# An attention stage moved from column tiles to 64x64 tiles of TensorE, two head pairs at a time

## The chip, the cores and the metric

One NeuronCore of one Trainium2 chip runs the whole kernel in one launch. The metric is the device time of that core in microseconds (us); smaller is better. The kernel before takes 602.62 us as the median of 3 runs (602.19 to 602.64).

## The reference

```python
S = q.shape[2]                               # q, k, v: (4, 12, 448, 64) float32
scores = q @ k.T / sqrt(64) - log(S)
attn = 1 / (1 + exp(-scores))                # a sigmoid: no sum over keys
attn_out = attn @ v
x = attn_out, tokens as rows                 # (1792, 768)
xn = x / sqrt(mean(x * x) + 1e-6) * rms_g
g, val = xn @ w_gate, xn @ w_val             # 768 -> 1536
out = (silu(g) * val) @ w_out                # 1536 -> 768
```

## The kernel before, in words

The kernel has three stages: attention (with the normalisation of its result), a gated feed-forward layer, and the output projection. Products run in float16 with each float32 operand split into a high part and a low part ("hi" and "lo"); three products (hi hi, hi lo, lo hi) then stand for one float32 product. The feed-forward stage uses Strassen-like sums of blocks, which is why a normalised activation is needed in seven combined forms (slots 0 to 6). Only the product of attention weights and v is done in float32 by TensorE itself. Each float32 matmul of the program shows as two MATMUL instructions in the trace.

**Attention.** The work unit is a pair of heads (24 pairs: 4 batches of 6). `load_qk` (L190, L191) brings q and k of a pair as 128 partitions by 7 chunks by 64; `load_v` (L199) brings v into slots with zero blocks between them. VectorE (DVE in the trace) makes hi (`qk_hi`, L204) and lo (`qk_lo`, L209) side by side, so that a 128-column chunk holds [lo | hi] of q and [hi | lo] of k. The chunks are transposed, for the first three pairs by TensorE against an identity (L224, evicted at L229 by VectorE and L231 by ScalarE), for the others by a DMA transpose on the SP queue (L214). After this, partitions 0 to 63 hold one part of the head dimension and 64 to 127 the other. `q_up` (L241) copies q's hi part to the lower partitions of a third plane whose upper half is zero.

`scores` (L258) handles a pair in four groups g. A 64-key block of a head is two matmuls over all 128 rows: one adds hi lo and lo hi at once (the two parts are stacked along the rows), one is hi hi against the zero half. Each matmul fills 64 of the 128 output partitions, and two of them on the two column halves of TensorE belong together. Groups 0 to 2 have 8 matmuls, group 3 has 4, so a pair has 28. One sigmoid on ScalarE (ACT, L260) evicts a group from PSUM. `av` (L271) multiplies with v, two float32 matmuls per group, again on the two column halves. After group 3 ScalarE evicts the result twice, squared (L280) and scaled by rms_g (L281), and VectorE later adds up the squares (L284).

**Order.** The program order is written out by hand: scores of two groups, then `av` of the two groups before them. Scores have two PSUM buffers. Between them `run_later` spends a budget (0.75 of VectorE per call, 0.18 of ScalarE) on queued parts: the adds of squares, `norm` (L302 sums, L307 to L323 a reciprocal square root, L329 spreads it, L332 scales, L336 and L341 split into hi and lo, L352 block sums) and the splitting of the first weights (`split_w`). What the budget has not reached at the end of attention stays in a list; parts beyond the last 33 (`N_NORM`) are issued at once ahead of the first feed-forward product, the last 33 between the products (`LEFT`).

```python
for n in range(0, len(todo) + 2, 2):
    for i, g in todo[n : n + 2]:
        scores(i, g)
        for part in FILL[g]:
            part(i)
        run_later()
    for i, g in todo[max(n - 2, 0) : n]:
        av(i, g)
        run_later()
while len(later) > N_NORM:
    later.pop(0)[0]()
```

Of the kernel before, what the change touches and what calls it, by code (L numbers as in the profile page):

```python
# [16 lines left out]
SQ = 2.0**6  # L17
# [7 lines left out]
def attention_then_swiglu(  # L25
# [27 lines left out]
    MID = S // P  # L53
    NG = MID + 1
# [15 lines left out]
    SPLIT_AT = 10  # L70
    ON_PE = 3
# [21 lines left out]
    NV = 10  # L93
    A_WORDS = 5 * 2 * S + 3 * NV * D + 4 * S
    B_WORDS = 2 * S + 3 * NCC * S + 3 * NK * S
# [23 lines left out]
    LDW, TW = 2 * NSLOT * D, 3 * NSLOT * D  # L119
    ld_b = [words(xc_room, XW + n * LDW, 2, NSLOT, D) for n in range(4)]  # L120
    nat_b = [words(xc_room, XW + 4 * LDW + n * LDW, 4 * NSLOT, D, dt=F16) for n in range(2)]
    nat_hi = [t[:, 1:-1].rearrange("p (t u) d -> p t u d", t=2)[:, :, 0::2] for t in nat_b]
    t_b = [words(xc_room, XW + 6 * LDW + n * TW, 3, NSLOT, P, dt=F16) for n in range(3)]
    at0 = 0
    a_b = [words(room, at0 + n * 2 * S, 2, S) for n in range(5)]
    at0 += 10 * S
    v_b = [words(room, at0 + n * NV * D, NV, D) for n in range(3)]
    at0 += 3 * NV * D
    sq_b = [words(room, at0 + n * S, S) for n in range(2)]
    at0 += 2 * S  # L130
    acc_b = [words(room, at0 + n * S, S) for n in range(2)]
    at0 += 2 * S
    diag_b = [words(room, at0 + n * S, S) for n in range(2)]
    at0 += 2 * S
# [46 lines left out]
    pairs = [(b, hp) for b in range(B) for hp in range(NPAIR)]  # L181
    at, pav = {}, {}

    def rows_of(src, i, order):
        b, hp = pairs[i]
        return src[b, 2 * hp : 2 * hp + 2].rearrange("h s d -> (h s) d").rearrange(order, p=P)

    def load_qk(i):
        t = ld_b[i % 4]
        nc.sync.dma_start(t[:, 0], rows_of(q, i, "(p c) d -> p c d"))  # L190
        nc.sync.dma_start(t[:, 1], rows_of(k, i, "(p c) d -> p c d"))  # L191

    def load_v(i):
        b, hp = pairs[i]
        t = v_b[i % 3].rearrange("p (j n) d -> p j n d", j=2)
        src = v[b, 2 * hp : 2 * hp + 2].rearrange("j (r c) d -> r j (c d)", c=NSLOT)
        for n in range(2):
            dst = t[64 * n : 64 * n + 64, :, 1 - n : 5 - n].rearrange("p j n d -> p j (n d)")
            nc.sync.dma_start(dst, src[:, :, MID * n * D : (MID * n + 4) * D])  # L199

    def qk_hi(i):
        nc.vector.tensor_scalar(nat_hi[i % 2], ld_b[i % 4], SQ, None, ALU.mult)  # L204

    def qk_lo(i):
        for t in range(2):
            lo = nat_b[i % 2].rearrange("p (t c l) d -> p t c l d", t=2, l=2)[:, t, :, t]
            stt(lo, ld_b[i % 4][:, t], SQ, nat_hi[i % 2][:, t], ALU.mult, ALU.subtract)  # L209

    def transpose(i):
        if i < ON_PE:
            return
        nc.sync.dma_start_transpose(  # L214
            out=t_b[i % 3][:, 0:2].rearrange("p t c r -> p (t c) r"),
            in_=nat_b[i % 2].rearrange("p u d -> p (u d)"),
        )

    def transpose_here(i, t, space, engines):
        nat = nat_b[i % 2].rearrange("p (t c l) d -> p t c (l d)", t=2, l=2)  # L220
        ps = space()
        for c in range(NSLOT):
            half_, at = divmod(c, MID + 1)
            nc.tensor.matmul(ps[half_][:, at * P : at * P + P], nat[:, t, c], ident16, start=True, stop=True)  # L224
        for half_, engine in enumerate(engines):
            n = MID + 1 - half_
            o = t_b[i % 3][:, t, half_ * (MID + 1) : half_ * (MID + 1) + n].rearrange("p c r -> p (c r)")
# [5 lines left out]
    def on_pe(i):  # L233
        if i < ON_PE:
            for t in range(2):
                transpose_here(i, t, lambda: [bank("tr") for _ in range(2)], (nc.vector, nc.scalar))
            credit[0] -= 1.1

    def q_up(i):
        T = t_b[i % 3]  # L240
        nc.vector.tensor_copy(T[:D, 2], T[D:, 0])  # L241

    def scores(i, g):

        T = t_b[i % 3]
        n = 1 if g == MID else 2
# [12 lines left out]
        a = at[i, g] = a_b[(i * NG + g) % 5]  # L259
        nc.scalar.activation(  # L260
            a[:, :n], ps[:, :n, :S], AF.Sigmoid, bias=bias_s, scale=1.0 / (math.sqrt(D) * SQ * SQ)
        )

    def av(i, g):
        b, hp = pairs[i]
        a = at.pop((i, g))
        if g == 0:
            pav[i] = bank("av")
        ps = pav[i]
        for j in range(2):  # L270
            nc.tensor.matmul(  # L271
                ps[64 * j : 64 * j + 64, :S],
                v_b[i % 3][:, NG + j if g == MID else 1 + 5 * j + g],
                a[:, 0 if g == MID else j],
                start=(g == 0),
                stop=(g == MID),
            )
        if g == MID:
            sq = sq_b[i % 2] if hp else acc_b[b % 2]
            nc.scalar.activation(sq, ps[:, :S], AF.Square)  # L280
            nc.scalar.activation(x_b[b % 3][:, hp], ps[:, :S], AF.Copy, scale=g_sb[:, hp : hp + 1])  # L281
            if hp:
                adds.extend([(wait, 0.0)])
                adds.append((lambda: tt(acc_b[b % 2], acc_b[b % 2], sq, ALU.add), 0.53))  # L284
            del pav[i]
# [4 lines left out]
    def norm(b):  # L290
# [4 lines left out]
        d = diag_b[odd][:TB]  # L295
# [144 lines left out]
    PARTS = ((0, 0), (0, 1), (1, 0))  # L440
# [275 lines left out]
    def ahead_by(n, part, cost=0.0):  # L716
        def run(i):
            if i + n < len(pairs):
                part(i + n)
                credit[0] -= cost  # L720

        return run

    FILL = (
        (ahead_by(1, on_pe), ahead_by(2, transpose)),
        (ahead_by(1, q_up, 0.4), ahead_by(5, load_qk)),
        (ahead_by(3, qk_hi, 0.53), ahead_by(2, load_v)),
        (ahead_by(3, qk_lo, 1.1),),
# [6 lines left out]
    for t in v_b:  # L735
        nc.vector.memset(t[:, NG : NG + 2], 0.0)
    for t in t_b:
        nc.vector.memset(t[D:, 2], 0.0)
# [186 lines left out]
```

## Time and profile before

| what | value |
|---|---|
| median of 3 runs | 602.62 us |
| the profiled execution: its own time | 603.15 us |
| its span in the profile | 601.3 us |
| end of the last `av` matmul (attention ends) | about 156.9 us |
| granted TensorE clock over the span | 1.00 |

PE is TensorE's matmuls, PEld its weight loads, DVE VectorE, ACT ScalarE, SP the queue that issues most DMAs. A row "xN | busy, mean" gives how many instructions a group has, the time that at least one of them ran, and the mean duration of one. Matmuls overlap, so a mean duration of 353 ns says nothing of the distance from one to the next; that is read from a stretch in which they stand back to back.

### The profile page before, as it was taken

The page shows a single profiled execution, that of the slowest core. Times are in us where ns is not written, and L with a number is a line of the kernel's source. Part 1 is how long each engine was busy: PE and PEld are TensorE (multiplying, and loading weights), DVE is VectorE, ACT ScalarE, POOL GpSimd, SP SyncE. Part 2 cuts the span into 40 slices and gives each one's busy share as a digit, 9 for nine tenths or more (in the row PEclk, how much of TensorE's full clock was granted, in tenths as well). Part 3 has the DMA queues.
Part 4 walks back from the last instruction along what each step waited for, and adds up shares of the span by engine and source line. Part 5 has one row for each costly group of instructions (what it writes and reads, how often), then busy time and mean ns, then how long its engine had stood idle before and what let it go on. Part 6 is the DMA issues. An engine that isn't in the chain of part 4 may idle for free.

```text
span 601.3 us, 9197 instructions
## 1 busy us (share of the span) xinstructions
PE 591.6 (98%) x3604; PEld 319.4 (53%) x3604; DVE 481.2 (80%) x763; ACT 265.0 (44%) x400; POOL 0.7 (0%) x6
## 2 busy tenths in 40 slices
PE   7999999999999999999999999999999999999997
PEld 5445454554455555555555555555556666666664
DVE  7696897986698998887887888878789997767651
ACT  5787887987553332323324324324232254222020
POOL 0000000000000000000000000000000000000000
PEclk9999999999999999999999999999999999999999
DMA  9999999972000330230320312303355014121112
GB/s 233 253 226 260 242 197 230 247 166 66 0 2 2 105 106 18 88 106 0 106 77 28 106 41 66 106 0 106 105 214 207 1 36 97 27 52 38 30 40 52
DMA packets 78747, 61.35 MB, mean 102 GB/s; under 512 B 42864, under 2 KB 77168, under 8 KB 78704
## 3 DMA queue, kind: packets, MB, share of 16 engines
q1 hardware_dynamic: 78384, 60.38, 39.2%
q8 instruction: 28, 0.46, 0.3%
q10 hardware_dynamic: 320, 0.39, 0.2%
q14 instruction: 15, 0.12, 0.1%
HBM read 45.62 MB, written 5.51 MB: 85 GB/s over the span
## 4 chain that ended last, share of the span: by engine, by line
PE 92%; ACT 3%; DVE 2%; DMA 2%; issue 1%; SPq 0%; ACTq 0%; DVEq 0%
PE cc L453 14%; PE cd L453 13%; PE ca L453 13%; PE o L542 12%; PE av L271 10%; PE sc L258 9%; PE cb L453 7%; PE oc L629 4%; PE od L629 4%; PE oa L629 4%; PE ob L629 2%; ACT room L260 1%; DMA room<-in_v_dram 1%; DMA xc<-in_k_dram 1%; ACT xc L336 1%
## 5 line engine op out<-in xcount | busy, mean ns | idle before, releaser
L453 PEld LDWEIGHTS <-wr 128*128 128x128 f16 x1512 | 147.8, 98 | 138.7 <-issue 1.2
L260 ACT ACTIVATE room<-sc,bias_s 128x896 f32<-128x896 f32 x96 | 83.9, 921 | 18.9 <-PE sc L258 18.5
L453 PE MATMUL ca<-xc,wr 128*128 128x448 f16 x432 | 89.6, 352 | 0.0
L271 PE MATMUL av<-room 128*64 128x448 f32 x384 | 80.7, 539 | 0.0
L258 PE MATMUL sc<-xc 128*64 128x448 f16 x672 | 74.0, 353 | 2.2 <-ACT room L260 1.1
L453 PE MATMUL cd<-xc,wr 128*128 128x448 f16 x324 | 67.2, 352 | 0.0
L453 PE MATMUL cc<-xc,wr 128*128 128x448 f16 x324 | 67.2, 352 | 0.0
L258 PEld LDWEIGHTS <-xc 128*64 128x64 f16 x672 | 40.7, 110 | 42.3 <-issue 25.4
L542 PE MATMUL o<-xc,room 128*128 128x384 f16 x354 | 58.3, 326 | 0.0
L481 ACT ACTIVATE room<-ca 128x448 f32<-128x448 f32 x24 | 13.0, 542 | 84.6 <-PE ca L453 84.6
L542 PEld LDWEIGHTS <-room 128*128 128x128 f16 x354 | 34.6, 98 | 22.9
L453 PE MATMUL cb<-xc,wr 128*128 128x448 f16 x216 | 44.8, 352 | 0.0
L271 PEld LDWEIGHTS av<-room 128*64 128x64 f32 x384 | 28.8, 137 | 27.1 <-issue 21.5
L429 DVE SCALAR_TENSOR_TENSOR wr<-wr 128x768 f16<-128x768 f32 (+1 forms) x48 | 39.1, 850 | 0.1
L508 ACT ACTIVATE room<-room 128x448 f32<-128x448 f32 x24 | 13.8, 576 | 53.4 <-DVE room L507 53.4
L426 ACT ACTIVATE wr<-wr 128x768 f16<-128x768 f32 (+1 forms) x48 | 34.2, 755 | 4.9 <-DVE wr L423 4.9
L476 DVE TENSOR_TENSOR room<-room,cb 128x448 f32<-128x448 f32 x24 | 14.9, 620 | 16.9 <-PE cb L453 16.8
L209 DVE SCALAR_TENSOR_TENSOR xc<-xc 128x448 f16<-128x448 f32 x48 | 27.8, 619 | 0.4
L381 DVE SCALAR_TENSOR_TENSOR wr<-wr 128x768 uint32<-128x768 uint32 x28 | 26.8, 957 | 0.8
L380 DVE SCALAR_TENSOR_TENSOR wr<-wr 128x768 uint32<-128x768 uint32 x28 | 26.8, 956 | 0.6
L469 ACT ACTIVATE room<-ca 128x448 f32<-128x448 f32 x24 | 13.0, 544 | 30.9 <-PE ca L453 25.2
L423 DVE TENSOR_TENSOR wr<-wr 128x384 f32<-128x384 f32 x48 | 25.6, 554 | 0.9
(145 smaller groups left out, 705.4 us busy)
## 6 DMA issues: line engine op xcount, KB each, us to landing
wr<-in_moe_w_gate_dram SPq DMA_DIRECT2D x36, 256.0 KB, 3.2
wr<-in_moe_w_val_dram SPq DMA_DIRECT2D x36, 256.0 KB, 3.9
room<-in_v_dram SPq DMA_DIRECT2D x48, 128.0 KB, 4.0
xc<-in_q_dram SPq DMA_DIRECT2D x24, 224.0 KB, 3.5
xc<-in_k_dram SPq DMA_DIRECT2D x24, 224.0 KB, 3.4
out_dram<-room SPq DMA_DIRECT2D x49, 96.0 KB, 2.2
wr<-in_moe_w_out_dram SPq DMA_DIRECT2D x6, 768.0 KB, 4.4
xc<-in_moe_w_out_dram SPq DMA_DIRECT2D x5, 768.0 KB, 6.3
```

The source lines that it names most:

```text
L209: stt(lo, ld_b[i % 4][:, t], SQ, nat_hi[i % 2][:, t], ALU.mult, ALU.subtract)
L258: nc.tensor.matmul(o, m, r, start=(w == 0), stop=(w == 1))
L260: nc.scalar.activation(a[:, :n], ps[:, :n, :S], AF.Sigmoid, bias=bias_s, scale=1.0 / (math.sqrt(D) * SQ * SQ))
L271: nc.tensor.matmul(ps[64 * j : 64 * j + 64, :S], v_b[i % 3][:, NG + j if g == MID else 1 + 5 * j + g], a[:, 0 if g == MID else j], start=( ...
L380: lambda: stt(b, r[:, :, 0], 29, b, ALU.logical_shift_right, ALU.bitwise_or),
L381: lambda: stt(b, r[:, :, 1], 0xC0000000, b, ALU.bitwise_and, ALU.bitwise_or),
L423: first.append((lambda o=o, f0=f0, f1=f1: tt(wf[:, o], wf[:, f0], wf[:, f1], ALU.subtract), 0.6))
L426: nc.scalar.activation(t[:, 0, s], wf[:, s], AF.Copy, scale=SW)
L429: stt(t[:, 1, s], wf[:, s], SW, t[:, 0, s], ALU.mult, ALU.subtract)
L453: nc.tensor.matmul(ps, w[:, l, b, c], xc[n, a][:, r, c], start=(not more and c == 0 and m == 0), stop=(c == NK - 1 and m == 2), skip_group ...
L542: nc.tensor.matmul(ps[:, :HALF], h[c, t // NTOK][:, l, t % NTOK * P : t % NTOK * P + P], wo[c][:, r, e * HALF : e * HALF + HALF], start=(c ...
L629: nc.tensor.matmul(ps[:, :HALF], a[x](m, l), b[y](m, r), start=(not more and m == 0 and n == 0), stop=(m == NFC // 2 - 1 and n == 2), skip ...
```

## The change

A unit is now two pairs of heads (12 units, 7 key chunks each, 84 steps in place of 96). Partitions 0 to 63 of q, k and v hold pair 0, partitions 64 to 127 pair 1; hi and lo are separate planes, and inside a chunk the two heads stand side by side, so that after the transposes a head's 64 dimensions fill one half of the partitions. A step issues 12 score matmuls of 64 rows by 64 columns (three products by two heads by two pairs) and 4 float32 `av` matmuls of the same size. Four matmuls in a row fall on the four quarters of TensorE; heads (score) or pairs (av) are the row halves, and these write different PSUM banks. The zero blocks of v and the copies of `q_up` are gone.

```diff
+    PARTS = ((0, 0), (0, 1), (1, 0))
-    def scores(i, g):
-        for j in range(2):
-            for w in range(2):
-                r = T[:, 2 * w, :, 64 * j : 64 * j + 64]
-                for half_ in range(2):
-                    cols = slice(64 * half_, 64 * half_ + 64)
-                    if g == MID and half_ != j:
-                        continue
-                    o = ps[cols, 0 if g == MID else j, :S].rearrange("p (c r) -> p c r", c=NSLOT)
-                    m = T[:, 1, MID if g == MID else g + NG * half_, 64 * j : 64 * j + 64]
-                    nc.tensor.matmul(o, m, r, start=(w == 0), stop=(w == 1))
+    def scores(u, c):
+        for n, (l, m) in enumerate(PARTS):
+            for j in range(2):
+                rows = slice(64 * j, 64 * j + 64)
+                for r in range(2):
+                    cols = slice(PB * r, PB * r + PB)
+                    o = ps[cols, j, :S].rearrange("p (c r) -> p c r", c=NSLOT)
+                    nc.tensor.matmul(
+                        o, T[rows, 1, l, c, cols], T[rows, 0, m, :, cols], start=(n == 0), stop=(n == 2)
+                    )
...
+        for r, ps in enumerate(pav[u]):
+            rows = slice(PB * r, PB * r + PB)
+            for j in range(2):
+                nc.tensor.matmul(
+                    ps[64 * j : 64 * j + 64, :S],
+                    v_b[u % 2][rows, j, c],
+                    a[rows, j],
...
+        evictions.extend((square, copy))
```

Around this: the four evictions of a unit (square and copy for two pairs) are issued one by one, each behind a `scores` or `av` (`run_evictions(1)`). Loads, hi, lo and transposes of q and of k are separate steps of a unit (`FILL`), two units ahead; `load_v` loads each value once. The first two units (four pairs, before: three) are transposed by TensorE, hi and lo apart; the first unit's loads come first, q before k. The hi copies of the normalisation of batch 1 go from ScalarE (15 of 448 columns) to VectorE (5 of 1344). The split of the second weights is queued at step 30, and weights from the third on are not loaded during attention:

```diff
-            if n < 8 or n % 4 == 0:
+            if True and loads and loads[0][0] < 2:
                 run_load()
-            if n == SPLIT_AT:
+            if n in SPLIT_AT:
...
+            if b == 1:
+                return [(lambda: nc.vector.tensor_copy(xc[n, slot][:, 0], f), 0.95)]
```

`N_NORM`, `LEFT` and both later stages are as before.

## Rows read from the trace of the kernel before

**Rows 1.** The page, part 1: busy time of each engine.

```profile
PE 591.6 (98%) x3604; PEld 319.4 (53%) x3604; DVE 481.2 (80%) x763; ACT 265.0 (44%) x400; POOL 0.7 (0%) x6
```

**Rows 2.** Busy time by stretch; last columns: granted clock, DMA share, GB/s.

```profile
0.00:16.90 16.90, 12.55 (x106) 8.73 (x108) 13.47 (x29) 8.85 (x13) 0.70 (x6) 1.00 0.95 238
16.90:156.90 140.00, 139.05 (x1043) 70.10 (x1043) 109.75 (x200) 117.31 (x172) 0.00 (x0) 1.00 0.89 199
...
30.00:60.00 30.00, 29.83 (x232) 14.98 (x228) 23.69 (x54) 24.80 (x35) 0.00 (x0) 1.00 1.08 244
```

**Rows 3.** The chain of waits, 15 to 30 us: start, length, what.

```profile
21.91 1.51 PE sc L258 x16
23.43 1.50 PE av L271 x8
```

**Rows 4.** Groups of instructions from 16.9 to 156.9 us.

```profile
L271 PE MATMUL av<-room 128*64 128x448 f32 x376 | 79.0, 539 | 0.0
L258 PE MATMUL sc<-xc 128*64 128x448 f16 x636 | 69.5, 353 | 0.9 <-ACT room L260 0.7
L260 ACT ACTIVATE room<-sc,bias_s 128x896 f32<-128x896 f32 x68 | 66.9, 1011 | 16.0 <-PE sc L258 15.5
L258 PEld LDWEIGHTS <-xc 128*64 128x64 f16 x636 | 38.5, 110 | 39.0 <-issue 24.4
L271 PEld LDWEIGHTS av<-room 128*64 128x64 f32 x376 | 28.2, 137 | 26.7 <-issue 21.1 <-ACT room L260 0.7
...
L260 ACT ACTIVATE room<-sc,bias_s 128x448 f32<-128x448 f32 x23 | 15.0, 651 | 0.0
...
L204 DVE TENSOR_SCALAR xc<-xc 128x896 f16<-128x896 f32 x20 | 12.5, 623 | 0.3
L336 ACT ACTIVATE xc<-room 128x448 f16<-128x448 f32 x21 | 12.3, 597 | 0.9 <-DVE room L352 0.8
...
L241 DVE COPY xc<-xc 64x896 f16<-64x896 f16 x22 | 8.6, 389 | 8.9 <-DMA xc<-xc 8.3
```

**Rows 5.** ScalarE in order of time: start, length, what.

```profile
70.78 1.92 ACT L260 ACTIVATE room<-sc,bias_s 128x896 f32<-128x896 f32 x2
...
73.02 0.58 ACT L280 ACTIVATE room<-av 128x448 f32<-128x448 f32 x1
73.45 0.68 ACT L281 ACTIVATE room<-av,g_sb 128x448 f32<-128x448 f32 x1
73.96 0.63 ACT L336 ACTIVATE xc<-room 128x448 f16<-128x448 f32 x1
```

**Rows 6.** The start in order of time: PE, then DVE, then ACT.

```profile
6.51 1.47 PE L258 MATMUL sc<-xc 128*64 128x448 f16 x8 [0.80 <-DVE xc L229]
...
5.17 1.29 DVE L229 CAST xc<-tr 128x512 f16<-128x512 f32 x2
...
7.37 0.63 DVE L204 TENSOR_SCALAR xc<-xc 128x896 f16<-128x896 f32 x1 [0.50 <-DMA xc<-in_k_dram]
8.04 1.16 DVE L209 SCALAR_TENSOR_TENSOR xc<-xc 128x448 f16<-128x448 f32 x2
...
14.09 0.63 DVE L204 TENSOR_SCALAR xc<-xc 128x896 f16<-128x896 f32 x1 [1.16 <-DMA xc<-in_k_dram]
...
3.86 0.58 ACT L759 ACTIVATE xc<-xc 128x448 f16<-128x448 f32 x1 [1.62 <-DMA xc<-in_k_dram]
```

**Rows 7.** SP's transposes: issue time min/median/max in ns, first and last start.

```profile
L214 SPq DMA_TRANSPOSE xc<-xc x21: 1378/2697/3816, 16.1 to 136.5; - x21
```

**Rows 8.** The end of attention in order of time: PE, then DVE.

```profile
156.90 1.88 PE L453 MATMUL ca<-xc,wr 128*128 128x448 f16 x9
...
163.41 0.99 PE L329 MATMUL rinv<-room,ones 112*128 112x448 f32 x2 [0.51 <-DVE room L323]
...
157.59 0.63 DVE L284 TENSOR_TENSOR room<-room 128x448 f32<-128x448 f32 x1 [2.43 <-ACT room L280]
158.58 1.56 DVE L341 TENSOR_TENSOR room<-room 128x1344 f16<-128x1344 f32 x1 [0.36 <-ACT room L336]
160.05 0.15 DVE L307 TENSOR_SCALAR m<-ssq 112x4 f32<-112x4 f32 x1
```

More of the change, by code (lines that the diff above doesn't have):

```diff
@@ L69, in attention_then_swiglu @@
     WARM = 9
-    SPLIT_AT = 10
-    ON_PE = 3
+    SPLIT_AT = (10, 30)
+    ON_PE = 2
+    MID = 3
     SLOT = 0.75
@@ L178, in attention_then_swiglu @@
     tt = nc.vector.tensor_tensor
-    pairs = [(b, hp) for b in range(B) for hp in range(NPAIR)]
     at, pav = {}, {}
[L184 to L199, printed above, removed]
@@ L203, in qk_hi, with rows_of @@
[L203 to L212, printed above, removed]
+    PARTS = ((0, 0), (0, 1), (1, 0))
+    def rows_of(src, u):
+        b, n = divmod(u, NPAIR // 2)
+        return [
+            src[b, 4 * n + 2 * r : 4 * n + 2 * r + 2].rearrange("j (p c) d -> p j (c d)", p=PB) for r in range(2)
+        ]
@@ new lines, in load, with load_qk, load_v, halves @@
+    def load(src, dst, u):
+        for r, rows in enumerate(rows_of(src, u)):
+            nc.sync.dma_start(dst[PB * r : PB * r + PB].rearrange("p j c d -> p j (c d)"), rows)
+    def load_qk(u, t):
+        load((q, k)[t], ld_b[u % 2][:, t], u)
+    def load_v(u):
+        load(v, v_b[u % 2], u)
+    def halves(u, t, l):
+        return nat_b[u % 2][:, t, l].rearrange("p c (j d) -> p j c d", j=2)
+    def qk_hi(u, t):
+        nc.vector.tensor_scalar(halves(u, t, 0), ld_b[u % 2][:, t], SQ, None, ALU.mult)
@@ L260, in scores, with av @@
         nc.scalar.activation(
-            a[:, :n], ps[:, :n, :S], AF.Sigmoid, bias=bias_s, scale=1.0 / (math.sqrt(D) * SQ * SQ)
+            a, ps[:, :, :S], AF.Sigmoid, bias=bias_s, scale=1.0 / (math.sqrt(D) * SQ * SQ)
         )
[L264 to L279, printed above, removed]
+    def av(u, c):
+        a = at.pop((u, c))
+        if c == 0:
+            pav[u] = [bank("av") for _ in range(2)]
+        for r, ps in enumerate(pav[u]):
+            rows = slice(PB * r, PB * r + PB)
+            for j in range(2):
+                nc.tensor.matmul(
+                    ps[64 * j : 64 * j + 64, :S],
+                    v_b[u % 2][rows, j, c],
+                    a[rows, j],
+                    start=(c == 0),
+                    stop=(c == NSLOT - 1),
+                )
+        if c == NSLOT - 1:
+            for r, ps in enumerate(pav.pop(u)):
+                evict(u, r, ps)
@@ L290, in norm, with run_evictions @@
+    def run_evictions(n):
+        for part in evictions[:n]:
+            part()
+        del evictions[:n]
+    evictions = []
     def norm(b):
@@ L714, in at_once, with ahead_by, run, next_v @@
         return [x for x in parts if x[0] is not wait]
[L716 to L719, printed above, removed]
+    def ahead_by(n, part, *t, cost=0.0):
+        def run(u):
+            if u + n < NU:
+                part(u + n, *t)
                 credit[0] -= cost
         return run
+    K, Q = 1, 0
+    def next_v(u):
+        if 0 < u < NU - 1:
+            load_v(u + 1)
     FILL = (
[L725 to L728, printed above, removed]
+        (ahead_by(2, qk_hi, K, cost=0.53),),
+        (ahead_by(2, qk_lo, K, cost=1.0),),
+        (ahead_by(2, transpose, K),),
+        (ahead_by(1, on_pe, K), next_v, ahead_by(2, qk_hi, Q, cost=0.53), ahead_by(4, load_qk, K)),
+        (ahead_by(2, qk_lo, Q, cost=1.0),),
+        (ahead_by(1, on_pe, Q), ahead_by(2, transpose, Q), ahead_by(4, load_qk, Q)),
+        (),
     )
@@ L764, in two_banks, with hi_on_act @@
             return [ps[:, n] for n in range(2)]
-        transpose_here(0, 0, two_banks, (nc.vector, nc.scalar))
-        transpose_here(0, 1, two_banks, (nc.vector, nc.scalar))
-        q_up(0)
-        for part in (qk_hi, qk_lo):
-            part(1)
-        load_qk(3)
-        todo = [(i, g) for i in range(len(pairs)) for g in range(NG)]
+        def hi_on_act(u, t):
+            nc.scalar.activation(halves(u, t, 0), ld_b[u % 2][:, t], AF.Copy, scale=SQ)
+        qk_hi(0, Q)
+        hi_on_act(0, K)
@@ new lines, in attention_then_swiglu @@
+        transpose_here(0, Q, 0, two_banks, (nc.vector, nc.scalar))
+        qk_lo(0, Q)
+        transpose_here(0, K, 0, two_banks, (nc.vector, nc.scalar))
+        qk_lo(0, K)
+        transpose_here(0, Q, 1, two_banks, (nc.vector, nc.scalar))
+        transpose_here(0, K, 1, two_banks, (nc.vector, nc.scalar))
+        for t in (K, Q):
+            qk_hi(1, t)
+            qk_lo(1, t)
+            transpose(1, t)
+            load_qk(2, t)
+        run_load()
+        run_load()
+        for t in (K, Q):
+            load_qk(3, t)
```

132 lines of the change are left out of this document (59 added, 73 removed).

## The prediction

> **What bounds the kernel now.** I read the shares first: PE is busy 98% of the span [rows 1]. The busy times by stretch then separate the stages: from 16.9 us to the end of attention at 156.9 us PE is busy for 139 of 140 us, ScalarE for 117, VectorE for 110, at a DMA share of 0.89, and the granted clock is 1.00, the 2.4 GHz level [rows 2]. So TensorE sets the pace of attention and ScalarE is next. The chain of waits alternates between scores and `av` with nothing between them [rows 3]; it gives the true cost of a matmul: 16 score matmuls in 1.51 us are 8 rounds of two column tiles at 189 ns; 8 `av` instructions in 1.50 us are 4 rounds at 375 ns. That two tiles share a round is seen, not assumed: the mean duration is 353 ns [rows 4], and yet one starts every 94 ns. In the dense stretch 636 score instructions times 94.4 ns and 376 `av` instructions times 187.5 ns [rows 4] make 130.5 us; the other 9.5 us are the normalisation's small matmuls and waits.
>
> **The change, part by part.**
>
> *Rounds on TensorE.* Before: 24 pairs x 28 scores x 94.4 ns = 63.4 us and 24 x 16 x 187.5 ns = 72.0 us, together 135.4. After: 84 steps, each with 12 score matmuls and 4 float32 matmuls (8 instructions). No row of this kernel shows two row tiles at work together, so the price of a round of four is bounded. Below: it streams the same 448 columns as a round of two, 189 and 375 ns. Above: only the column halves overlap, which doubles both. I take the lower end, because two tiles with separate streams already run at full rate [rows 3], and four streams over 64 partitions read as much as two over 128. That is 84 x (3 x 189 + 2 x 375) = 84 x 1.317 = 110.6 us: **-24.8 us** on the path. About 15.8 of it are the scores (three half-row products in place of two whole ones, of which one was half zeros), 9.0 the `av` products, whose fourth group ran with half a block of zeros.
>
> *Start.* Before, the first scores start at 6.51 us, and by 16.9 us 36 scores (672 less 636) and 8 `av` instructions are done, 4.9 us of work [rows 4, 6]. After, the first scores need q and k of two pairs. k of unit 0 is the third and fourth 224-KB transfer, and the fourth transfer of the kernel before has landed at 7.3 us, where `qk_hi` (L204) stops waiting [rows 6]. Then come in a row: hi on ScalarE, about 1 us (0.58 for half as many columns [rows 6]), the transposes, an eviction of 0.65 (half of 1.29 for two), lo 1.16, transposes and a last eviction: first scores at about 12 us. Unit 1's k is the eighth such transfer; the eighth landed at 14.1 us [rows 6], so its hi, lo and transposes hold TensorE again until about 21 us, with 4.9 us of work done by then (six steps of scores, two of `av`). That is **+4 us** (0 to +8). The four DMA loads of unit 0 and its two of v are issued ahead of everything else, so the weights and later loads only move back.
>
> *Waits inside the dense stretch.* Sigmoids have the same number of columns, but 84 instructions instead of 96. A second one adds 0.91 us to the first (1.92 less 1.01) [rows 4, 5], so 12 fewer starts save about 2 us. The hi copies of batch 1 leave ScalarE: 15 times some 0.5 us (0.59 with overlap [rows 4]) is 7.5, and 6 copies slide behind attention, 3 us. So 117 becomes about 105 us, in a stretch that shrinks from 140 to about 118: 89% in place of 84%. The evictions add 0.43 and 0.51 us each (starts 73.02, 73.45, 73.96 [rows 5]), four per unit, 1.9 us in a row of slots whose room is small: a round of two steps lasts 2.63 us on TensorE and takes 1.8 of sigmoid. The scores have two PSUM buffers, so a sigmoid late by more than half a microsecond stops TensorE. What is queued behind the evictions is the next sigmoid, and behind that the scores two steps on. I take 0.25 us per unit, **+3 us**; the bounds are -4 (the present 9.5 us shrink as the normalisation waits less) and +12 (1 us a unit).
>
> *VectorE, SP and DMA.* `q_up` goes, 8.6 us in this stretch [rows 4], and five casts come, each 1.5 times the 0.62 of L204 [rows 4], 4.7 us; VectorE stays under TensorE (about 103 of 118 us), so I cost both at nothing. If that cover goes, the late part is qk, with two units of slack. The DMA moves about 29 MB in place of 31.9 (238 GB/s x 16.9 and 199 x 140 [rows 2]): one transpose, the double v slots and the third weights fall away. At the share of before that is 128 us of DMA time in 139; 1.08 was held for 30 us [rows 2], so it is close but hidden. SP's 20 transposes hold its queue 2.7 us each [rows 7], 54 us; loads of the next units stand behind them, and both have 9 to 12 steps (12 us or more) until they are needed.
>
> *Behind attention.* The budget is spent per call of `run_later`: 192 calls before, 168 after. Following the credits through the loop, 35 parts are left before, and 44 after. So ahead of the first product stand eleven parts (two adds, a block sum, six hi copies, two lo) instead of two. TensorE's order holds the spread of the reciprocal root (L329), which waits for VectorE's chain from L307 on; it waits 0.51 us now, with 0.63 + 1.56 us of leftover ahead of that chain [rows 8]. One more add, one block sum and one lo are 0.63 + 1.55 + 1.56 = 3.7 us, and the second square lands an eviction later. The wait moves from 0.5 to about 4.5: **+4 us** (+0.5 if VectorE's chain overlaps ScalarE's, +6).
>
> *The rest* of the kernel is untouched. Sum: -24.8 + 4 + 3 + 4 = -13.8 us. The profiled execution took 603.15, which gives 589.3; the median of the runs shown lies 0.5 below that execution, so **589 us**. With the terms at their near ends together it is about 577, at their far ends 601.
>
> **The rivals.**
>
> *Slower: row halves do not overlap.* In `scores` and `av` the two row halves then take turns, and the change does not do what it says. Rounds cost 378 and 750 ns: +110.6 us, less some 4 of waits that get covered: about 695 us. The break-even lies where rounds are 13.8/110.6, an eighth, longer than 189 and 375 ns. Against it: row halves write different banks, as the column halves of `av` write different partitions. For it: no 64-row matmul stands in the trace. The Trainium skill, page "TensorEngine Tiling (Array Packing)", section "Tiling Modes", lists 64x64 as four tiles that work in parallel; no run here shows it yet. Chance 0.10.
>
> *Weight loads become the bound.* A round of two needs two loads in 189 ns, a round of four needs four. The 636 loads keep PEld busy 38.5 us, 61 ns each [rows 4]; four at that rate are 242 ns, so a score round costs 53 more: 84 x 3 x 53 = 13.4 us, 602 to 603, no change. `av` loads at 75 ns (28.2 / 376) would still hide. Against it: PEld is idle for 24.4 and 21.1 us there with nothing but its queue to wait for [rows 4], and the 61 ns include overlap. The Trainium skill, page "TensorE: Matmul & The Clock Gate", section "Part 3: Packing small matmuls — row/col tiling", measured 3.07 times for four row tiles, not 4. By that figure both kinds of round would be 1.3 times as long, and as an estimate the time would be about 622. By the trace, two column tiles lose nothing (two scores per 189 ns), so it is not borne out there. Chance 0.08.
>
> *ScalarE becomes the bound.* Each unit's four evictions push the sigmoids back by a full microsecond: +12 in place of +3, and with a start at +7 this is about 601. For it: 16.0 us of ScalarE's idle time is waiting for scores, so today it has room that the change takes [rows 4]. Against: the evictions are spread over four calls. Chance 0.08.
>
> **How the numbers follow.** The forecast has 0.74 and its time is the prediction. About 0.03 of that case lies under 577 and as much over 601; the second and third rivals end at 601 to 603, so 577 to 603 holds about 0.82 and leaves out the 695 and the tails. A measurement of this kernel tells about 0.2%, 1.2 us, from no change: faster is below 601.4, with nearly all of the forecast and half of the ScalarE rival, 0.79; within it 0.05; slower 0.16.
>
> **What would show it.** Right: four score matmuls per about 190 ns in a dense stretch, attention ending near 139 us instead of 156.9, first scores near 12 us, ScalarE at nearly 90% busy, the wait ahead of the last root's spread about 4 us. Wrong: rounds of 240 ns or 380 ns; score matmuls waiting for the sigmoid in every unit; a dense stretch with waits for DMA transposes or v; or a feed-forward stage that starts without the wait.

## The result, and the profile after

The changed kernel takes 606.41 us (median of 4 runs, 605.74 to 607.37), the kernel before beside it 602.48 (4 runs, 602.19 to 602.64). The ratio is 1.0067, with a 95% interval of 1.005 to 1.0085: **slower by 0.7%**, where 589 us and faster was forecast. The profiled execution of after took 607.37 us with a span of 605.6, so the spans differ by 605.6 - 601.3 = 4.3 us.

The busy times of the page, as in [rows 1], say little: TensorE is busy for 9 us less, and yet the span is longer.

```profile
PE 582.7 (96%) x4242; PEld 317.6 (52%) x4242; DVE 475.3 (78%) x739; ACT 256.4 (42%) x375; POOL 0.7 (0%) x6
```

First the part that came true. The chain of waits of after, in the first dense stretch and up to the first stall (start, length, what), answers to [rows 3]:

```profile
26.75 1.50 PE av L263 x16
28.26 1.13 PE sc L248 x24
...
36.34 1.05 PE sc L248 x21
37.39 4.35 DMA room<-in_v_dram
```

24 score matmuls in 1.13 us are 6 rounds of four at 189 ns, and 16 `av` instructions in 1.50 us are 4 rounds at 375 ns, as fast as rounds of two were before. The work of TensorE fell as forecast. But the last of the four lines is new: the chain leaves TensorE and goes through a load of v. The order of time on TensorE shows this stall and those after it; the bracket at the end is the idle time before a group and what ended it:

```profile
12.22 4.81 PE L248 MATMUL sc<-xc 64*64 64x448 f16 x48 [0.19 <-ACT xc L229]
...
41.78 2.23 PE L263 MATMUL av<-room 64*64 64x448 f32 x14 [1.67 <-DMA room<-in_v_dram]
...
55.07 2.06 PE L263 MATMUL av<-room 64*64 64x448 f32 x6 [3.17 <-DMA room<-in_v_dram]
...
70.04 2.35 PE L263 MATMUL av<-room 64*64 64x448 f32 x14 [0.38 <-DMA room<-in_v_dram]
...
126.30 0.59 PE L263 MATMUL av<-room 64*64 64x448 f32 x2 [1.34 <-ACT room L283]
...
154.71 1.88 PE L466 MATMUL ca<-xc,wr 128*128 128x448 f16 x9
157.13 0.92 PE L314 MATMUL ssq<-ones,room 128*112 128x1 f32 x8 [0.54 <-DVE room L286]
...
164.86 1.83 PE L341 MATMUL rinv<-room,ones 112*128 112x448 f32 x2 [3.39 <-DVE room L335]
166.48 3.57 PE L466 MATMUL cc<-xc,wr 128*128 128x448 f16 x9
```

Loads of v are late three times; the wait at 126 us is for an eviction on ScalarE. Attention ends at 154.71 us, where the first feed-forward product starts, against 156.90 before [rows 8] and about 139 in the forecast. From there to the end of the span it is 605.6 - 154.71 = 450.9 us, against 601.3 - 156.90 = 444.4. So attention gave 2.2 us and the rest cost 6.5: together the 4.3.

Stretches of the span, as in [rows 2] (busy time of PE, PEld, DVE, ACT and POOL, then granted clock, DMA share, GB/s); first before, then after:

```profile
20.00:80.00 60.00, 59.67 (x458) 29.96 (x454) 46.62 (x85) 49.68 (x72) 0.00 (x0) 1.00 1.04 241
80.00:140.00 60.00, 59.38 (x446) 31.15 (x444) 52.53 (x102) 51.83 (x77) 0.00 (x0) 1.00 0.97 210
```

```profile
20.00:80.00 60.00, 53.61 (x694) 28.44 (x690) 40.41 (x75) 41.58 (x55) 0.00 (x0) 0.94 1.14 220
80.00:140.00 60.00, 56.49 (x790) 30.76 (x786) 53.69 (x84) 53.03 (x73) 0.00 (x0) 1.00 1.02 197
...
54.00:61.00 7.00, 5.93 (x42) 3.50 (x46) 2.42 (x5) 2.02 (x4) 0.00 (x0) 0.53 1.13 246
61.00:68.00 7.00, 7.00 (x98) 4.17 (x94) 4.50 (x21) 4.30 (x6) 0.00 (x0) 0.99 1.10 239
...
163.60:170.40 6.80, 5.54 (x13) 2.33 (x14) 4.05 (x10) 2.07 (x4) 0.00 (x0) 0.50 0.00 0
```

Three things are to be seen. The DMA engines carry less per second at a higher share (220 GB/s at 1.14, 241 at 1.04 before): a byte became dearer. TensorE, VectorE and ScalarE are all less busy in 20 to 80 us than before, so none of them is full there. And after the idle times of 3.17 and 3.39 us the granted clock is 0.5, the 1.2 GHz level, for about 7 us each time: 42 matmul instructions stand in 54 to 61 us (5.93 of it busy), 98 in the next 7. Before, the clock stayed at 1.00 throughout.

SP's transposes are held a little longer than in [rows 7] (issue time minimum, median, maximum in ns):

```profile
L213 SPq DMA_TRANSPOSE xc<-room x20: 1527/3038/4986, 19.1 to 127.7; - x20
```

The DMA view of the first 160 us shows the dearer bytes, first before, then after (packets, MB, share of 16 engines; then KB each and the median us from issue to landing):

```profile
q1 hardware_dynamic: 57808, 31.67, 87.6%
...
xc<-in_q_dram SPq DMA_DIRECT2D x24, 224.0 KB, 3.5
...
xc<-xc SPq DMA_TRANSPOSE x21, 5.0
```

```profile
q1 hardware_dynamic: 52528, 30.42, 94.6%
...
xc<-in_q_dram SPq DMA_DIRECT2D x24, 224.0 KB, 4.8
...
room<-in_v_dram SPq DMA_DIRECT2D x24, 224.0 KB, 4.4
...
xc<-room SPq DMA_TRANSPOSE x20, 6.3
```

For 1.25 MB less the packets take 0.946 x 160 = 151 us of DMA time in place of 0.876 x 160 = 140. In the trace's packet records the median packet of 1792 bytes (the rows of q, k and v; before, those of q and k) takes 126 ns, before 74; the mean is 125 ns, before 94.

### The profile page after: what moved, and what is told of

Same layout as the page of the kernel before. It is cut to its first block, busy times and chain, and to the rows that moved or that the text cites. A ratio compares the mean times of both kernels' runs of the same rounds, so it can differ in the third digit from the quotient of the medians.

```text
span 605.6 us, 10344 instructions
## 1 busy us (share of the span) xinstructions
PE 582.7 (96%) x4242; PEld 317.6 (52%) x4242; DVE 475.3 (78%) x739; ACT 256.4 (42%) x375; POOL 0.7 (0%) x6
## 4 chain that ended last, share of the span: by engine, by line
PE 88%; ACT 5%; DMA 3%; DVE 1%; issue 1%; SPq 0%; ACTq 0%
PE cc L466 14%; PE ca L466 13%; PE cd L466 13%; PE o L555 12%; PE av L263 8%; PE cb L466 6%; PE sc L248 6%; PE oc L642 4%; PE od L642 4%; PE oa L642 4%; ACT room L252 3%; DMA room<-in_v_dram 2%; PE ob L642 2%; PE rinv L341 1%; DMA xc<-in_k_dram 1%
## 5 line engine op out<-in xcount | busy, mean ns | idle before, releaser
L252 ACT ACTIVATE room<-sc,bias_s 128x896 f32<-128x896 f32 x84 | 82.6, 1018 | 29.1 <-PE sc L248 28.5
L263 PE MATMUL av<-room 64*64 64x448 f32 x672 | 82.7, 550 | 7.6 <-DMA room<-in_v_dram 5.2
L248 PE MATMUL sc<-xc 64*64 64x448 f16 x1008 | 68.3, 366 | 2.1 <-ACT room L252 1.8
L466 PE MATMUL cc<-xc,wr 128*128 128x448 f16 x324 | 68.9, 359 | 0.0
L248 PEld LDWEIGHTS <-xc 64*64 64x64 f16 x1008 | 37.8, 110 | 32.7 <-issue 21.6
L263 PEld LDWEIGHTS av<-room 64*64 64x64 f32 x672 | 30.2, 135 | 34.5 <-issue 18.2
L208 DVE SCALAR_TENSOR_TENSOR room<-xc,room 128x448 f16<-128x448 f32 x48 | 27.8, 620 | 0.6
```

The lines of the kernel that those rows point to most:

```text
L208: stt(halves(u, t, 1)[:, j], ld_b[u % 2][:, t, j], SQ, halves(u, t, 0)[:, j], ALU.mult, ALU.subtract)
L248: nc.tensor.matmul(o, T[rows, 1, l, c, cols], T[rows, 0, m, :, cols], start=(n == 0), stop=(n == 2))
L252: nc.scalar.activation(a, ps[:, :, :S], AF.Sigmoid, bias=bias_s, scale=1.0 / (math.sqrt(D) * SQ * SQ))
L263: nc.tensor.matmul(ps[64 * j : 64 * j + 64, :S], v_b[u % 2][rows, j, c], a[rows, j], start=(c == 0), stop=(c == NSLOT - 1),)
L466: nc.tensor.matmul(ps, w[:, l, b, c], xc[n, a][:, r, c], start=(not more and c == 0 and m == 0), stop=(c == NK - 1 and m == 2), skip_group ...
```

## The experiments

The changed kernel loads each 224-KB piece of q, k or v into 64 partitions (one pair), by two runs of 1792 bytes for each. Before, a piece of q or k went into all 128; v went into 64 already, in pieces of 128 KB with runs of 1024 bytes. The theory after the result was: these transfers cost the DMA engines more, v and transposed q or k come late, the clock falls behind the longer stalls, and the leftover of the normalisation costs the rest. Rivals were: v is issued too late, whatever a byte costs; SP's queue holds it up; ScalarE is the new limit. All results (the kernel before measured 602.57 to 602.73 beside them; "attention ends" is the start of the first `ca` in the profile):

| run | median us | ratio, 95% interval | attention ends |
|---|---|---|---|
| e1_whole | 603.32 | 1.0015 (1.0 to 1.0031) | 151.07 |
| e2_v_ahead | 608.33 | 1.0095 (1.0066 to 1.0124) | 155.68 |
| e3_before_half | 627.15 | 1.0409 (1.0389 to 1.0428) | 179.97 |
| e4_slot | 605.14 | 1.0048 (1.003 to 1.0066) | 156.90 |
| e5_v_pool | 614.33 | 1.0181 (1.0143 to 1.022) | 162.16 |
| e6_whole_v_pool | 605.93 | 1.0061 (1.0026 to 1.0095) | 152.53 |
| e7_whole_vw_pool | 617.86 | 1.0262 (1.0244 to 1.0281) | 166.07 |
| e8_whole_vw_pool_slot | 612.06 | 1.0133 (1.0077 to 1.0189) | 164.94 |
| e9_no_v | 599.07 | 0.9943 (0.9924 to 0.9963) | 146.93 |
| e10_whole_late_w | 602.22 | 0.9995 (0.9966 to 1.0024) | 149.96 |
| e11_whole_pe3 | 604.77 | 1.003 (1.0012 to 1.0047) | 152.94 |
| e12_whole_late_w_pe3 | 607.35 | 1.0071 (1.0051 to 1.0092) | 153.72 |
| e13_no_v_no_sq | 597.94 | 0.9911 (0.9887 to 0.9935) | 146.47 |
| e14_no_v_slot | 596.23 | 0.9893 (0.9877 to 0.9908) | 147.90 |
| e15_whole_slot | 600.10 | 0.9964 (0.994 to 0.9987) | 152.29 |
| e16_whole_spread_slot | 595.09 | 0.987 (0.9852 to 0.9887) | 146.59 |

In the profiled executions of e1, e9, e15 and e16 the granted clock was 0.5 from about 8 to 15 us as well, where after kept 1.00. Unit 1's transposes still ended between 23.0 and 24.3 us there (24.0 in after), so the ends of attention can be compared to about a microsecond.

### Whole-partition loads of q and k (and v with them)

A unit's heads are regrouped so that one transfer fills all 128 partitions. The loads of rms_g and of the first weights permute their rows to match.

```diff
-            src[b, 4 * n + 2 * r : 4 * n + 2 * r + 2].rearrange("j (p c) d -> p j (c d)", p=PB) for r in range(2)
+            src[b, 4 * n + 2 * j : 4 * n + 2 * j + 2].rearrange("r s d -> (r s) d").rearrange("(p c) d -> p (c d)", p=P)
+            for j in range(2)
```

> The changed kernel, but each load of q, k or v writes all 128 partitions (two neighbouring heads in one transfer of 224 KB, one run per partition) as in the kernel before; the pairs of a unit are then made of other heads, so the rows of w_gate, w_val and rms_g are permuted in their loads (those become half-partition loads). Theory L (loads into half the partitions are slow, 1792-byte packets take 126 ns instead of 74, and the DMA paces attention): packets back at about 74 ns, waits of av for v gone, no fall of the clock in attention, attention ends near 142 us instead of 154.7, time 591 to 597. Theory O (v is only issued too late): av still waits for v, 603 to 607. Theory A (ScalarE sets the pace): packets faster, but waits move to the sigmoid, 602 to 606.

3.1 us less than the change as given. The DMA view of 0 to 160 us and the first two stalls:

```profile
q1 hardware_dynamic: 52864, 30.42, 84.8%
...
xc<-in_q_dram SPq DMA_DIRECT2D x24, 224.0 KB, 4.3
...
room<-in_v_dram SPq DMA_DIRECT2D x24, 224.0 KB, 3.5
```

```profile
51.14 1.29 PE L264 MATMUL av<-room 64*64 64x448 f32 x5 [1.77 <-DMA room<-in_v_dram]
66.17 0.96 PE L264 MATMUL av<-room 64*64 64x448 f32 x2 [1.71 <-DMA room<-in_v_dram]
```

The same bytes now take 0.848 x 160 = 136 us in place of 151, the 1792-byte packets are back at 74 ns, and attention ends 3.6 us earlier. But v is still late, by 4.0 us in all (5.2 in after), and the time misses the 591 to 597 of theory L by far; it lies where theory O had it. Dear bytes are a part of the loss, not the whole.

### v issued a unit earlier

```diff
-        load(v, v_b[u % 2], u)
+        load(v, v_at(u), u)
+    spare_v = [words(room, ROOM - 2 * NCC * S + m * UW // 2, 2, NSLOT, D) for m in range(3)]
```

> The changed kernel with three more places for v, so that v of units 2 to 6 is loaded a whole unit earlier; nothing else. Theory O: the three long waits for v (at 41.8, 55.1 and 70.0 us) vanish with the fall of the clock, 596 to 600. Theory L: v is in time but the transfers are as slow; q, k or transposes come late in its place, and half or less of that is gained, 601 to 606.

1.9 us slower than after. The waits for v are gone, and others stand in their place (waits of TensorE from 20 to 150 us):

```profile
PE sc L253 <- DMA xc<-room: 8.5, 3, 3.6
```

Now the transposed q and k come late, 8.5 us in place of 5.2 for v. The time is above the ranges of both theories. So v was not merely issued too late: when it is put forward, something else on the same queue and the same DMA engines is put back.

### The kernel before with its loads cut in two

```diff
-        nc.sync.dma_start(t[:, 0], rows_of(q, i, "(p c) d -> p c d"))
+            for n in range(2):
+                nc.sync.dma_start(t[64 * n : 64 * n + 64, m], rows[64 * n : 64 * n + 64])
```

> The kernel before with each load of q and k cut into two transfers of 64 partitions; nothing else. Theory L: 1792-byte packets go from a median of 74 ns to about 110 to 130, the DMA time of the first 160 us from 141 to over 150 us of 16 engines, and the time goes up by 2 to 12 us, as the DMA share there is over 1 for 100 us already. Theory O or A: packets may be slower, but the time stays within 0.3% of 602.5.

24.5 us slower than before (627.15 against 602.63), far outside what either side expected. The issues of q and k on SP's queue (minimum, median, maximum ns), first before, then e3:

```profile
L190 SPq DMA_DIRECT2D xc<-in_q_dram x24: 328/574/1107, 0.7 to 122.0; - x24
```

```profile
L193 SPq DMA_DIRECT2D xc<-in_q_dram x48: 495/592/1224, 0.7 to 149.4; - x48
L193 SPq DMA_DIRECT2D xc<-in_k_dram x48: 482/595/1335, 2.0 to 150.6; - x48
```

An issue costs about as much for half the bytes, so SP is held 96 x 0.59 = 57 us in place of some 24 (24 x 0.574, and 24 of k at 0.420). SP had little room for that: its DMA instructions take 52.8 of the 60 us from 20 to 80 before and 54.9 in e3, and from 80 to 140 us 48.7 before and 55.3 in e3. That the 24.5 us come from the added issues is likely, but no run tests it by itself.

The DMA share was lower than before (0.88 in 20 to 80 us), and the median 1792-byte packet stayed at 74 ns. The median hides a part, though: the mean rose from 94 to 109 ns, and 26% of these packets took over 100 ns, against 12% before, 68% in after and 10% in e1. So loads into 64 partitions made some packets slow here too, but far fewer than in after. And the form alone does not do it: v before and the weights of e1 go into 64 partitions by two runs of 1024 bytes for each, and their median packet took 46 ns (53 ns for the weights of after, which fill all 128). What e1 took away is the whole form of the load of q, k and v; its parts were not tried singly, and which of them makes a packet dear stays open.

### A larger budget for the parts of the normalisation

```diff
-    SLOT = 0.75
+    SLOT = 0.86
```

> The changed kernel with the budget of VectorE per call raised from 0.75 to 0.86, so that 168 calls spend what 192 did; nothing else. If the parts left over at the end of attention make the wait ahead of the spread (3.39 us) and the half clock behind it, that wait falls to about 0.5 us, the clock stays up and the time falls by 4 to 6 us, to 600 to 602. Rival: VectorE gets more work while it is behind anyway, and the wait moves into attention: 604 to 608.

605.14 us, 1.3 less than after. The start of the feed-forward stage on TensorE:

```profile
156.90 1.88 PE L466 MATMUL ca<-xc,wr 128*128 128x448 f16 x9
159.69 0.95 PE L314 MATMUL ssq<-ones,room 128*112 128x1 f32 x8 [0.90 <-DVE room L286]
165.29 0.99 PE L341 MATMUL rinv<-room,ones 112*128 112x448 f32 x2 [1.23 <-DVE room L335]
```

The wait ahead of the spread is 1.23 us in place of 3.39, and the `rinv` behind it takes 0.99 us in place of 1.83: the clock stays at the higher level. From the end of attention to the end of the span it is 603.3 - 156.9 = 446.4 us, 4.5 less than after. The wait ahead of the spread is 2.2 us shorter and the one ahead of `ssq` 0.4 longer (0.54 in after), so 1.8 are waits; the other 2.7 fit the clock, since the 5.54 us that TensorE is busy from 163.6 to 170.4 us in after would be 2.8 at full clock. Attention itself ended 2.2 us later, with v late by 7.9 us in all, and so the time lies in the range of the rival (604 to 608).

### Another queue for v and the weights

e5 puts v of the changed kernel on GpSimd's queue; e6 does it with whole-partition loads, e7 moves the attention stage's weights too, e8 adds the budget of e4.

```diff
-        load(v, v_b[u % 2], u)
+        load(v, v_b[u % 2], u, nc.gpsimd)
```

> The changed kernel with v loaded from GpSimd's queue, which has nothing else to do, instead of SP's; the transfers are the same half-partition ones. Theory Q (SP's queue paces attention: from 10 to 80 us its issues stand back to back, and v stands behind transposes of 3 us each): 24 issues of 0.63 us leave it, waits for v vanish, q, k and transposes come earlier, 597 to 602. Theory L (the transfers' own speed into half the partitions): v comes earlier, but transposes are late in its place as when v was loaded ahead, 604 to 609.

> Whole-partition loads of q, k and v together with v on GpSimd's queue. Theory L and Q both hold in part, so that each alone uncovers the other: no wait for v or transposes of over 0.5 us in attention, its end near 143 to 146 us, 594 to 599. If neither is the pace (ScalarE or VectorE is): 601 to 604, as with whole-partition loads alone.

> As the run before, and the weights loaded during attention (two of twelve chunks, here cut into halves of partitions, 24 issues of 0.62 us) on GpSimd's queue too. Theory Q: SP has another 15 us less, start and middle of attention gain 1 to 4 us more, 591 to 597. Theory L: equal to the run before within 1 us.

> As the run before, with the budget of VectorE per call at 0.86 as in the earlier run with 0.86 alone. If the wait at the start of the feed-forward stage is independent of attention's loads, it gives 2 to 5 us more, as it gave 1.3 us alone with VectorE's work moved into a starved attention: 587 to 594. Rival: VectorE, then 90% busy, holds the squares and q/k up, no gain.

All are slower than the same kernel with v on SP's queue, and e5, e6 and e7 are above every range that was expected: e5 by 7.9 us, e6 by 2.6 over e1 (with runs spread from 602.73 to 610.65), e7 by 14.5 over e1, e8 by 12.0 over e15. e5's transposes land after 8.0 us (6.3 in after), and SP holds one of them for 8.47 us (start, length):

```profile
49.08 8.47 SPq L213 DMA_TRANSPOSE xc<-room  x1
...
54.04 1.33 PE L248 MATMUL sc<-xc 64*64 64x448 f16 x12 [5.21 <-DMA xc<-room]
```

In e5 and e6 no wait for v is left, and waits for the transposes stand in their place (10.0 and 3.4 us). So moving v off SP's queue is no cure; but as the second queue brings a loss of its own, these runs do not show that SP's queue has no part in v's lateness (its DMA instructions fill 53.5 of the 60 us from 20 to 80 in after, 52.8 before). Why loads from a second queue put the transposes back so far is open.

### No v at all

v of units 2 to 11 isn't loaded, everything else stays as in the changed kernel.

```diff
-        if 0 < u < NU - 1:
-            load_v(u + 1)
+        pass
```

> The changed kernel without the loads of v for units 2 to 11 (the first two units' v is used again, so these units' result is left out); it takes a third of the half-partition transfers away, about 20 us of DMA time, and one late load. Theory D (the DMA engines as a whole pace attention up to 75 us: 153 us of their time where TensorE has 111 us of rounds; whatever is moved to another place in the queue, something else comes late): no wait for a transfer over 0.5 us, no fall of the clock in attention, attention ends near 144 to 147, time 595 to 599. If the pace is set elsewhere (ScalarE, VectorE): above 602.

7.3 us less than after; attention ends 7.8 us earlier. The same windows as above:

```profile
20.00:80.00 60.00, 55.21 (x790) 29.65 (x783) 48.29 (x87) 48.84 (x67) 0.00 (x0) 1.00 1.12 225
80.00:140.00 60.00, 56.84 (x802) 30.59 (x805) 49.91 (x92) 51.27 (x70) 0.00 (x0) 1.00 0.70 143
```

The queue's DMA time in 160 us is 0.795 x 160 = 127 us, what the forecast took for all transfers. One DMA wait is left (1.68 us, for a transpose), and the clock is full from 20 to 140 us. So the loads of v, with what they make late and the clock that fell behind it, are worth 7 to 8 us of the attention stage. The time is just above the 595 to 599 that was expected.

### Later weights, a third unit transposed by TensorE

e10 (on e1) puts the second weights' loads off to step 32 and their split to step 44. e11 (on e1) transposes a third unit by TensorE, e12 does both.

```diff
-            if True and loads and loads[0][0] < 2:
+            if loads and loads[0][0] < (2 if n >= 32 else 1):
```

```diff
-    ON_PE = 2
+    ON_PE = 3
```

> Whole-partition loads of q, k and v, and the second weights' loads put off from steps 16 to 26 to step 32 and later, their split from step 30 to 44; the bytes are the same. Theory D: 9 us of DMA time leave the stretch before 65 us; the waits for v there (1.8, 1.7, 0.5 us) vanish with the short fall of the clock, 3 to 6 us under whole-partition loads alone: 597 to 600. Rival (v is late by its place in the queue alone): no more than 1 us, 602 to 604.

> Whole-partition loads, and the third unit too transposed by TensorE: two DMA transposes of 20 less, about 6 us of DMA time at 20 to 30 us, for 28 small matmuls (1.5 us of TensorE) and 8 evictions. Theory D: waits for v shrink by 2 to 3 us, price 1.5 to 2.5 us: 600 to 604. Rival: transposes are not what fills the DMA: 604 to 606.

> Both of these with whole-partition loads: 15 us of DMA time leave the first 65 us. Theory D: nothing in attention waits for a transfer; what is left are waits for ScalarE after 80 us and the start of the feed-forward stage: 597 to 601. Rival: no better than whole-partition loads alone, 602 to 605.

e10 stands at 602.22, in the range of its rival (602 to 604) and level with before, but its ten runs spread from 598.5 to 606.72. Its early stalls for v shrank to 0.38 and 0.32 us, and one of 2.27 us came at 95 us, behind the weights that had been put off. e11 is in the range of its rival too (604 to 606). No DMA wait is left on TensorE from 24 to 150 us, yet it isn't faster than e1: TensorE now waits for evictions of its transposes (2.8 us for those of VectorE, 0.6 in e1), and the granted clock fell at 34 to 38 us. e12 has the same waits, and its clock fell for twice as long (33 to 40 us); it is slower than either edit alone.

### The part of ScalarE

e13 is e9 without 20 of the 24 squares of ScalarE, e14 is e9 with the budget of e4.

```diff
-            nc.scalar.activation(sq, ps[:, :S], AF.Square)
+            if not hp:
+                nc.scalar.activation(sq, ps[:, :S], AF.Square)
```

> The run without v's later loads, and without 20 of ScalarE's 24 squares as well (the sums of squares are then taken over other data: v of the first units and the unsquared result; both left out of the result). ScalarE loses 20 x 0.43 = 8.7 us of about 100. Theory A (the other half of attention's loss is ScalarE's evictions holding sigmoids and PSUM banks up): the waits for L252 and L283 shrink by half or more, attention ends 3 to 6 us before 146.9, 593 to 596. Rival (they are set by the order PE and ScalarE wait for each other in, not by ScalarE's load): under 1.5 us, 597.5 to 600.

> The run without v's later loads (their result left out) with the budget per call at 0.86. If the loss at the start of the feed-forward stage is its own term: the wait ahead of the last spread from 3.4 to about 1 us, the clock stays up there, 593 to 596. Rival: VectorE's extra work delays q and k in attention as much: 598 to 601.

e13 ends attention 0.5 us before e9 and is 1.1 us faster, an amount within the spread of its runs (595.92 to 599.27) and in the range of its rival (597.5 to 600). The waits of scores for the sigmoid went from 2.8 us to 0.2; a wait of 2.2 us for a transpose came back. From 80 to 140 us, where no transfer was late in either, PE is busy 58.41 us in place of 56.84. So the 8.7 us of work that ScalarE lost (20 squares at 0.43) are worth 1 to 2 us, not the 12 of the rival. e14 is 2.8 us faster than e9, by the start of the feed-forward stage, as e4 had it.

### Putting it together

e15 is e1 with the larger budget. e16 adds two edits: the second weights are loaded one every fourth step, by the rule of the kernel before, with their split at step 40, and the hi copies of batch 0 move to VectorE too.

```diff
-            if True and loads and loads[0][0] < 2:
+            if loads and (loads[0][0] < 1 or loads[0][0] < 2 and n % 4 == 0):
...
-            if b == 1:
+            if b <= 1:
```

> Whole-partition loads of q, k and v and the budget at 0.86: the two gains add, 603.3 less 3 to 5 us, 598 to 600.5. Rival: no gain over whole-partition loads alone, 602 to 604.

> Whole-partition loads, budget 0.86, the second weights' loads one every four steps with their split from step 40, and the hi copies of batch 0 on VectorE too. If early bytes, ScalarE and the leftover are the three losses: 594 to 598, faster than both kernels. Rival: VectorE becomes the pace, 599 to 603.

e15 is 0.4% faster than before. e16 takes **595.09 us** (594.16 to 595.51), 7.6 less than the kernel before and 11.3 less than the change as given. Its DMA queue, its windows, its waits from 24 to 146 us, and the start of the feed-forward stage:

```profile
q1 hardware_dynamic: 52864, 30.42, 81.4%
```

```profile
20.00:80.00 60.00, 56.79 (x788) 30.91 (x780) 45.13 (x81) 48.77 (x64) 0.00 (x0) 1.00 1.04 231
80.00:140.00 60.00, 58.25 (x796) 31.05 (x790) 52.57 (x97) 49.28 (x64) 0.00 (x0) 1.00 0.86 196
```

```profile
PE av L264 <- DMA room<-in_v_dram: 1.4, 2, 0.7
PE av L264 <- DVE room L345: 1.0, 1, 1.0
PE sc L249 <- ACT room L253: 0.6, 1, 0.6
```

```profile
155.58 0.99 PE L342 MATMUL rinv<-room,ones 112*128 112x448 f32 x2 [1.78 <-DVE room L336]
```

The same bytes as in after, with attention 8.1 us shorter: what e9 got by leaving v out, e16 gets with v. The DMA share in 20 to 80 us is back at 1.04, the share of before. Against e15, the added edits bring the waits for v from 4.4 us to 1.4. e10 tried a near form of the first edit; the second was not run alone, so the 5.0 us between e15 and e16 can't be divided between them.

## Why the prediction was wrong

**Rounds on TensorE, -24.8: right.** Rounds of four take 189 and 375 ns, so the rivals with 695 us (row halves in turns) and 602 us (weight loads) fall. The Trainium skill, page "TensorE: Matmul & The Clock Gate", section "Part 3: Packing small matmuls — row/col tiling", has 3.07 times for four row tiles (of 32 rows); by the 189 ns of the chain, four tiles of 64 by 64 in a dense stream lose nothing here.

**Start, +4: mechanism right, size 2.9 us short.** First scores start at 12.22 us (about 12 forecast). But unit 1's transposes hold TensorE until 23.9 us, not 21, and what is done by then is as forecast: 72 scores and 16 `av` instructions, 3.4 + 1.5 = 4.9 us of work. So the term measured about +7, near the far end of its 0 to +8.

**"VectorE, SP and DMA: at nothing", and with it the +3 for waits in the dense stretch: the step that failed.** The prediction said "close but hidden", from 29 MB at the share of before, 128 us of DMA time. The bytes were right: 210 GB/s over the first 140 us are 29.4 MB. But they took 1.06 x 140 = 148 us (columns as in the stretches above):

```profile
0.00:140.00 140.00, 125.01 (x1594) 69.50 (x1598) 106.24 (x180) 103.69 (x140) 0.70 (x6) 0.98 1.06 210
```

Three things were wrong:

- The price of a byte was taken over from before, though the change halves the partitions that each load of q and k writes. 151 us were measured; at the price of before, 140 us for 31.67 MB, the 30.42 MB would have taken 134. The Trainium skill, page "SBUF — State Buffer", section "Door 1: The DMA port swizzle (why `[64,N]` ≈ `[32,N]`)", says that a transfer to 64 partitions reaches only half of the ports. That agrees with 126 ns against 74 for a packet in after, only in part with e3 (median 74 ns, mean 109 against 94), and not with the 1024-byte packets of v before and of the weights of e1, at a median of 46 ns each; it would have been a rule to weigh against the row.
- A mean over the stage was used where the stage has a crowded part. The DMA share was already 1.08 in 30 to 60 us before [rows 2] and 1.04 in 20 to 80. As an estimate, the same transfers in a dense stretch of 118 us in place of 140 would have needed 1.04 x 140 / 118 = 1.23 there; after reached 1.14. The weights are not to blame for the crowding: the diff takes away the condition `n < 8 or n % 4 == 0`, but 10 of their loads are issued from 20 to 80 us before and 9 in after. e16 puts off some of them and moves the hi copies as well, and the stalls for v shrink to 1.4 us.
- A stall was priced at its own length. Behind 3.17 us of idle time TensorE ran for about 7 us at 1.2 GHz.

The size of the whole is shown from two sides: without v attention ends 7.8 us earlier (e9), with the dear loads gone, the second weights later and two edits to VectorE's parts 8.1 us (e16). The dear loads alone are 3.6 of that (e1). How much of the rest is the DMA engines and how much SP's queue, which carries the same transfers, no run separates.

**Behind attention, +4: mechanism right, size short.** The wait ahead of the spread was put at about 4.5 us and is 3.39. With the 0.54 us ahead of `ssq` the waits grew by 3.4 us (3.93 against 0.51). But 6.5 us were lost there in all: the clock fell behind that wait too, worth some 2.8. With the wait at 1.23 us (e4) 4.5 of the 6.5 come back.

**The ScalarE rival, +12:** scores wait 1.8 us for the sigmoid in all of after, and in e13 8.7 us less work for ScalarE are worth 1 to 2 us. It falls.

**What stays open.** Attention was to end at 139 and ends at 146.6 even in e16; some 2 us of that are the start. From 24 to 146.5 us that kernel has 936 scores and 648 `av` instructions, 936 x 1.13 / 24 + 648 x 1.50 / 16 = 104.8 us of work, and 5.9 us of normalisation matmuls. So 11.8 of 122.5 us are lost, where before had 9.5 - 5.9 = 3.6 in its 140. The waits that the profile names make 3.7 of them (1.4, 1.0, 0.6, 0.4 and 0.3). A part of the rest lies in gaps that don't show as idle, since a matmul that is shown for 350 ns covers the end of a round of 189. A larger part lies in stretches in which only some of the four tiles work, which count as busy too. The timeline of e16 shows one:

```profile
105.89 0.94 PE L264 MATMUL av<-room 64*64 64x448 f32 x4
107.21 1.34 PE L264 MATMUL av<-room 64*64 64x448 f32 x10 [0.38 <-ACT room L284]
```

The four instructions are pair 0's product; pair 1's waits for its PSUM bank. So the two tiles of pair 1 stand still for the 1.3 us from 105.9 to 107.2, and 0.38 is shown. With 189 ns for each score instruction and 375 for each `av` instruction from their recorded starts, an estimate is that no tile works for 6.6 us of the 122.5 and one to three for another 11.7, worth 5.6 us of all four. What ends each of these gaps was not followed.

## What to carry to other kernels

When a change shortens the stage that hides the transfers, sum the DMA time anew for its most crowded part and at the price of the new loads (which partitions, how many issues), not at the mean share of the old stage. An idle time of 3.4 us on TensorE cost some 2.7 us more in granted clock, so an edit that shortens it pays twice. A layout that suits TensorE's tiles need not be the layout of the load: regrouping heads and permuting the weights' rows gave whole-partition loads of q, k and v with no more work for TensorE. And where several tiles work side by side, a busy TensorE may have half of them waiting: count the instructions against the time of a round.

## What the runs showed of the hardware

- Four tiles of 64 by 64 run a round over 448 columns in 375 ns (float32) and 189 ns (float16), the pace of rounds of two 128 by 64 tiles before, their weight loads hidden (PEld busy 37.8 us for 1008 score loads).
- The tiles of the two row halves can fall out of step: in e16 two score instructions start at 108.03 us, ahead of two `av` instructions that stand before them in the program and start at 108.39.
- Loads of 64 partitions by two runs of 1792 bytes took 126 ns a packet (median), whole-partition loads 74. In e3, at a lower DMA share, 64-partition loads of one run had a median of 74 and a mean of 109, against 94 before; 1024-byte runs into 64 partitions took 46 (median).
- An issue on SP's queue took about 0.6 us (median) for a load into 64 partitions, of 112 KB (e3), 128 KB (v before) or 224 KB (after) alike, and 0.39 to 0.57 for a whole-partition load of 224 KB (e1, and q and k before). A kernel with twice as many issues for q and k was 24.5 us slower.
- v on GpSimd's queue put the landing of the DMA transposes from 6.3 to 8.0 us, and single waits for them reached 10.4 us (e7).
